# Turning the last batch's q and k by DMA in a fused attention and feed-forward kernel

## The chip, the core and the metric

The program runs on one core of one Trainium2 chip. Its time is device microseconds from start to end of one execution. The kernel before takes 698.06 us, the median of 3 runs (697.01 to 699.1). The profile below is of one further execution, which took 696.34 us in all; the span from its first to its last recorded instruction is 694.5 us, and the 1.84 us between the two lie around the span.

## What is computed

Four batches of 8 heads, 576 positions, head size 64. A position bias goes through a small two-layer network; then softmax attention; the result is reshaped to 2304 tokens of 512 numbers and goes through a feed-forward layer of 2048 with a leaky activation.

```python
def _attn_ref(q, k, v, w1, b1, w2):          # q, k, v: (4, 8, 576, 64)
    scores = 1 / np.sqrt(D) * np.matmul(q, k.transpose(0, 1, 3, 2))
    x = (np.log1p(np.abs(rel)) / psi_i)[..., None]      # (576, 576, 1)
    bias = np.maximum(x @ w1 + b1, 0.0) @ w2             # (576, 576, 8)
    scores = scores + bias.transpose(2, 0, 1)[None]
    attn = np.exp(scores - np.max(scores, axis=-1, keepdims=True))
    attn = attn / (np.sum(attn, axis=-1, keepdims=True) + 1e-09)
    return np.matmul(attn, v)

def _moe_ref(x, w_in, w_out, alpha):         # x: (2304, 512)
    h = x @ w_in                              # 512 -> 2048
    g = np.maximum(h, 0.0) + alpha * np.minimum(h, 0.0)
    return g @ w_out                          # 2048 -> 512
```

## The kernel before

**Precision.** A float32 number is kept as two float16 planes, a rounded high part and the rest, and a product of two such numbers is three float16 matmuls (high by high, high by low, low by high). Weights, feed-forward inputs and, for batches 1 to 3, also q, k, v and the attention weights are held in this form. Batch 0 is computed in float32.

**Stages.** `bias_tile` (L472) makes the bias of 16 positions at a time and stores it to the scratch tensor `scr` in HBM. `weights` (L658) loads and splits the feed-forward weights. `qk_turn` (L569) loads q and k of one batch and one half of its heads as rows (positions on the partitions) and turns them, so that the head dimension lies on the partitions. `v_rows` (L620) loads and splits v. `unit` (L779) is the attention of one pair of heads and 256 or 320 positions: scores (L612), add the bias and take the maximum (L823, DVE), exponential (L826, ACT), normalise into planes (L836 or L837, then L839), turn them by DMA (L842), multiply by v (L876) and write the result into a feed-forward input tile `x` (L902, L904). `chunk` (L912) takes 256 tokens through the feed-forward layer: first product into PSUM tile `H` (L954, 24 matmuls), activation (L961 on ACT, L962 on DVE), planes of it (L965, L966 or L967), second product into `O` (L973, 12 or 6 matmuls), scale and store (L935 to L943).

**q and k of batches 1 to 3, before.** `load_rows` (L523) issues five DMAs each for q and k into buffers of the class `five` (7 slots, 128 x 1280 float32). `qk_scales` (L548) finds the largest magnitude of each, by DVE (L554) or by ACT (L555, whose element-wise result is junk and is put into the buffer that the turned q and k will fill); TensorE turns the two maxima (L464) and spreads them over the partitions (L466); eight small DVE instructions (L559 to L566) make a power-of-two scale of them. Then, for each of q and k and each of two pairs of heads, TensorE turns five blocks of rows in float32 (L586, a group of five) into one PSUM tile, ACT writes the scaled high plane from PSUM (L592) and DVE the low plane (L593) into the buffer `qk` (3 slots). That is four groups for one half of the heads and eight for a batch.

**Order.** Nothing is scheduled when the program is built: `ISSUE` lists all steps of the program in one sequence, with the engine for those that have a choice (a suffix .1 or .2), `SLOT` gives each buffer its slot, and `IDLE` says before which steps how many matmuls with a zero operand (L1025, "fillers") are put into TensorE's queue. Each engine executes its part of the list strictly in order. All DMAs but one are issued from SP's queue, so a DMA that waits for its data holds up every DMA behind it. TensorE alternates between attention and the feed-forward layer from the second batch on; a feed-forward chunk can run when all attention units of its tokens are done.

Of the kernel before, what the change touches and what calls it, by code (L numbers as in the profile page):

```python
# [10 lines left out]
F16 = mybir.dt.float16  # L11
# [8 lines left out]
P = 128  # L20
# [122 lines left out]
"""  # L143
IDLE = """
7:9 108:4 115:1 73:4 35:11 444:2 59:1 168:1 94:1 101:4 657:6 45:1 66:4 229:2 122:1 934:1 650:4 622:2 636:1 129:3 608:1 671:3 150:4 643:1 136:3 692:1
699:5 678:1 287:2 685:2 495:5 713:2 720:6 543:3 537:6 557:3 329:1 568:2 774:2 802:4 426:1
"""

# [929 lines left out]
```

## Time and profile before

| | |
|---|---|
| median of 3 runs | 698.06 us (697.01 to 699.1) |
| the profiled execution | 696.34 us, span 694.5 us |
| TensorE (PE) busy | 665.5 us, 96% of the span |
| VectorE (DVE) busy | 496.4 us, 71% |
| ScalarE (ACT) busy | 399.1 us, 57% |
| GpSimd (POOL) busy | 180.7 us, 26% |
| DMA, share of 16 engines | 77.5% |
| granted TensorE clock | 0.999 |

A busy share is a mean over stages. In this program the stages differ: in the first 180 us bias, weights and batch 0 are made, until some 590 us attention and feed-forward work are mixed, and the rest is feed-forward alone. So the profile is read by stretch, and for each stretch by the chain of waits. Matmuls overlap in the pipeline, so the mean time of one matmul row is longer than what it adds to the path; the pieces of the chain of waits show the latter.

### The profile page before, as it was taken

How to read it: one execution, taken by the hardware profiler on the slowest of the kernel's cores; microseconds unless marked ns; L12 is line 12 of the kernel's file. 1: busy time of each engine (PE TensorE's matmuls, PEld its weight loads, DVE VectorE, ACT ScalarE, POOL GpSimd, SP SyncE). 2: the span in 40 equal slices, each digit the busy share in tenths (PEclk: the TensorE clock that was granted, in tenths of full speed). 3: DMA queues.
4: the chain of work that ended last, by engine and by line, in shares of the span. 5: the costliest groups of instructions: out<-in, count | busy, mean ns of one | idle time of the engine just before them, and what ended most of it. 6: DMA issues, size and time to landing. Idle time of an engine off the chain costs nothing.

```text
span 694.5 us, 15288 instructions
## 1 busy us (share of the span) xinstructions
PE 665.5 (96%) x5737; PEld 421.7 (61%) x5737; DVE 496.4 (71%) x1208; ACT 399.1 (57%) x820; POOL 180.7 (26%) x244
## 2 busy tenths in 40 slices
PE   7998898999999999999999999999999999999997
PEld 2544444556666657666665766666666667666664
DVE  4999999998788878897786787867686564132221
ACT  3579999896756766656646665454565333222311
POOL 1445245441233122111214211302121131111120
PEclk9999999999999999999999999999999999999999
DMA  8999998868589999999998999799997863100000
GB/s 198 267 291 321 302 323 282 283 178 200 119 209 182 200 192 233 186 221 221 197 236 200 209 199 191 158 212 184 175 218 167 172 134 61 33 31 1 31 1 32
DMA packets 234342, 125.89 MB, mean 181 GB/s; under 512 B 202636, under 2 KB 202652, under 8 KB 234268
## 3 DMA queue, kind: packets, MB, share of 16 engines
q1 hardware_dynamic: 234136, 124.91, 77.5%
q8 instruction: 45, 0.74, 0.4%
q14 instruction: 29, 0.24, 0.1%
q10 hardware_dynamic: 132, 0.00, 0.0%
HBM read 73.88 MB, written 15.61 MB: 129 GB/s over the span
## 4 chain that ended last, share of the span: by engine, by line
PE 72%; DVE 12%; DMA 6%; issue 4%; ACT 3%; POOL 2%; SPq 0%; ACTq 0%; DVEq 0%; POOLq 0%
PE H L954 25%; PE O L973 24%; PE S L612 7%; PE A L876 6%; DMA at<-a 2%; PE A L884 2%; PE S L586 2%; PE S L503 1%; DVE fg L823 1%; DVE five L682 1%; DVE wout L682 1%; DVE qk L593 1%; DVE at L482 1%; PE S L855 1%; DMA five<-in_k_dram 1%
## 5 line engine op out<-in xcount | busy, mean ns | idle before, releaser
L954 PE MATMUL H<-x,win 128*128 128x256 f16 x1728 | 200.7, 273 | 0.7 <-DVE mg L962 0.5
L973 PE MATMUL O<-wout,mg 128*128 128x512 f16 x864 | 197.7, 379 | 0.3 <-DVE mg L966 0.3
L954 PEld LDWEIGHTS <-win 128*128 128x128 f16 x1728 | 166.5, 98 | 33.9 <-issue 6.8
L962 DVE SCALAR_TENSOR_TENSOR mg<-H,sm,mg 128x256 f32<-128x256 f32 x144 | 66.8, 479 | 105.7 <-ACT mg L961 105.5
L961 ACT ACTIVATE mg<-H,sm 128x256 f32<-128x256 f32 x144 | 64.8, 470 | 134.1 <-PE H L954 115.2
L973 PEld LDWEIGHTS <-mg 128*128 128x128 f16 x864 | 82.6, 98 | 92.5 <-issue 3.8
L826 ACT ACTIVATE fg<-fg,st 128x576 f32<-128x576 f32 x144 | 110.6, 769 | 29.0 <-DVE st L823 23.8
L823 DVE CUSTOM_DVE_ANT_0 fg<-S,fg 128x576 f32<-128x576 f32 x127 | 93.6, 751 | 15.7 <-PE S L612 14.6
L967 POOL TENSOR_TENSOR mg<-mg 128x512 f16<-128x512 f32 x41 | 50.1, 1222 | 114.1 <-ACT mg L965 45.2
L839 DVE SCALAR_TENSOR_TENSOR a<-fg,st,a 128x576 f16<-128x576 f32 x71 | 59.5, 840 | 19.8 <-POOL a L836 9.9
L836 POOL TENSOR_SCALAR a<-fg,st 128x576 f16<-128x576 f32 x41 | 32.8, 802 | 136.5 <-DMA at<-a 77.1
L612 PE MATMUL S<-qk 64*128 64x288 f16 (+1 forms) x696 | 56.6, 285 | 2.2 <-DVE qk L593 2.2
L876 PE MATMUL A<-at,five 128*64 128x256 f16 (+3 forms) x720 | 51.5, 288 | 0.6 <-DMA at<-cst 0.6
L829 POOL TENSOR_SCALAR st<-st 128x2 f32<-128x2 f32 (+1 forms) x54 | 17.3, 320 | 123.1 <-ACT fg L826 118.9
L612 PEld LDWEIGHTS <-qk 64*128 64x128 f16 (+1 forms) x720 | 33.0, 96 | 23.1 <-issue 17.7
L876 PEld LDWEIGHTS <-five 128*64 128x64 f16 (+1 forms) x720 | 36.1, 109 | 15.0 <-issue 11.9
L485 ACT ACTIVATE at<-cst 128x528 f32<-128x528 f32 (+17 forms) x54 | 33.8, 659 | 10.2 <-PE S L503 7.4
L503 PE MATMUL S<-at,w2b 128*32 128x79 f32 (+37 forms) x462 | 32.9, 334 | 5.5 <-ACT at L485 1.9
L1025 PE MATMUL H<-sm 128*128 128x512 f16 x121 | 36.3, 412 | 0.9 <-DVE sm L413 0.9
L965 ACT ACTIVATE mg<-mg 128x512 f16<-128x512 f32 x40 | 24.9, 624 | 17.9 <-DVE mg L962 6.6
L839 DVE SCALAR_TENSOR_TENSOR cst<-fg,st,cst 128x576 f16<-128x576 f32 x37 | 32.0, 864 | 3.0 <-ACT cst L837 3.0
L488 POOL TENSOR_SCALAR at<-cst,npsi 128x416 f32<-128x416 f32 (+15 forms) x28 | 23.1, 827 | 41.6 <-PE S L503 24.0
(158 smaller groups left out, 902.3 us busy)
## 6 DMA issues: line engine op xcount, KB each, us to landing
fg<-scr SPq DMA_DIRECT2D x64, 576.0 KB, 4.6
scr<-fg SPq DMA_DIRECT2D x36, 295.5 KB, 4.9
x<-in_moe_w_in_dram SPq DMA_DIRECT2D x11, 512.0 KB, 5.6
x<-in_moe_w_out_dram SPq DMA_DIRECT2D x10, 512.0 KB, 5.7
fg<-scr SPq DMA_DIRECT2D x32, 144.0 KB, 4.1
out_dram<-mg SPq DMA_DIRECT2D x18, 256.0 KB, 2.7
five<-in_q_dram SPq DMA_DIRECT2D x32, 128.0 KB, 3.8
five<-in_k_dram SPq DMA_DIRECT2D x32, 128.0 KB, 3.3
```

What stands on the lines that cost most here:

```text
L503: nc.tensor.matmul(ps.t[32 * gl:32 * gl + 32, c:n], lhsT=w2b, rhs=x, start=True, stop=True)
L612: return [(lambda a, dst=dst, zq=zq, zk=zk, i=i: nc.tensor.matmul(dst(a), lhsT=tr16(qt)[at, 0, pr, zq, lo:lo + n], rhs=tr16(qt)[at, 1, pr, ...
L823: V(lambda x=x, sl=sl, st=st, ls=ls: nc.vector.tensor_tensor_reduce(out=in_halves(ls[x]()), in0=halves(sl[x].t), in1=in_halves(ls[x]()), s ...
L826: A(lambda x=x, st=st, ls=ls: nc.scalar.activation(ls[x](), ls[x](), AF.Exp, bias=st.t[:, x:x + 1], scale=-1.0, accum_out=st.t[:, 2 + x:3 ...
L839: V(lambda x=x, rec=rec, ls=ls, a16=a16: nc.vector.scalar_tensor_tensor(a16.t[:, 640:640 + S], ls[x](), rec(), a16.t[:, 0:S], op0=ALU.mult ...
L876: nc.tensor.matmul(ps.t[64 * hh:64 * hh + 64, 0:w], lhsT=v5[0:hi, zv, n, 2 * pr + hh, :], rhs=at16(at)[0:hi, 5 * za + n, 320 * hh:320 * hh ...
L954: nc.tensor.matmul(hb.t[:, f, :], lhsT=win[:, fp, zw, kb, P * f:P * f + P], rhs=x[:, zx, kb, :], start=(n == 0), stop=(n == 11))
L961: A(lambda f=f: nc.scalar.activation(gf(f), hb.t[:, f, :], AF.Copy, scale=cu[:, f:f + 1]), 470, ky, [hb, t_sig], [(g, f)])
L962: V(lambda f=f: nc.vector.scalar_tensor_tensor(gf(f), hb.t[:, f, :], cs[:, f:f + 1], gf(f), op0=ALU.mult, op1=ALU.max), 475, ky, [hb, t_si ...
L967: ("POOL", 1210, lambda: nc.gpsimd.tensor_tensor(gv(1), g.t, gv(0), op=ALU.subtract))], ky, [g, (gg, 0)], [(gg, 1)], tag="g1", cont=True)
L973: nc.tensor.matmul(ob.t[:, t, :], lhsT=gg.t[:, zg, f, P * t:P * t + P], rhs=wout[:, fp, zw, f, :], start=(first and f == 0 and (zg, zw) == ...
L1025: nc.tensor.matmul(idle, lhsT=zero.broadcast_to((P, P)), rhs=zero.broadcast_to((P, 512)), start=True, stop=True)
```

## The change

For batch 3 alone, `qk_turn` no longer uses TensorE to turn q and k. The new `qk_planes` takes two more buffers of the class `five`, one for q and one for k, and lets ACT (L577) write the high plane and DVE (L578) the low plane from the rows as they were loaded, one instruction each of 128 x 1280 for q and for k. Ten DMA transposes (L582), five each, then turn blocks of 128 (or, the last one, 64) rows of these planes, 512 columns wide, into the buffer `qk`. The junk of the maximum on ACT (L555) goes into the plane buffer. For the two halves of the heads this is 40 TensorE transposes, 8 ACT and 8 DVE instructions of 128 x 576 less, and 4 ACT and 4 DVE instructions of 128 x 1280 and 20 DMAs in SP's queue more. The scale, the three products and the layout of `qk` stay as they were.

`ISSUE`, `SLOT` and `IDLE` are all new: the whole sequence differs, not only the rows of batch 3. The lines after the insertion are numbered 21 higher (L612 is L633, L842 is L863, L954 is L975, L973 is L994).

```diff
-0 2 9 10 3 11 4 13 12 15 5 14 19 104 106 6 7 107.1 8 16 205 206 193 105.2 108 113 114.1 20 21 22 111.2 17 71.1 194 112 23 115 24 25 48 207 26 70.2 27
...
-7:9 108:4 115:1 73:4 35:11 444:2 59:1 168:1 94:1 101:4 657:6 45:1 66:4 229:2 122:1 934:1 650:4 622:2 636:1 129:3 608:1 671:3 150:4 643:1 136:3 692:1
...
+20:13 108:7 664:1 35:1 45:3 671:2 657:1 168:1 73:4 52:1 66:5 80:3 629:3 122:6 87:3 650:1 615:3 608:3 143:2 636:3 129:4 150:2 692:8 643:4 727:3 699:3
...
-    def qk_scales(st, tr, key):
+    def qk_scales(st, tr, key, planes=None):
...
-            junk = lambda tr=tr, j=j: tr.t[:, j].rearrange("p a n -> p (a n)").bitcast(F16)[:, 0:1280]
+            junk = (lambda j=j: planes[j].t.bitcast(F16)[:, 0:1280]) if planes else (lambda tr=tr, j=j: tr.t[:, j].rearrange("p a n -> p (a n)").bitcast(F16)[:, 0:1280])
...
+    def qk_planes(st, tr, key):
+
+        planes = [Buf(c_stage) for _ in range(2)]
+        sc2, tok = qk_scales(st, tr, key, planes)
+        for j in range(2):
+            p5 = lambda j=j: planes[j].t.bitcast(F16).rearrange("p (r c z n) -> p r c z n", r=5, c=2, z=2)
+            src = lambda j=j: st[j].t.rearrange("p (r c n) -> p r c n", r=5, c=2)
+            sv = sc2[:, j:j + 1]
+            A(lambda p5=p5, src=src, sv=sv: nc.scalar.activation(p5()[:, :, :, 0], src(), AF.Copy, scale=sv), 1350, key, [st[j], tok], [(planes[j], 0)])
+            V(lambda p5=p5, src=src, sv=sv: nc.vector.scalar_tensor_tensor(p5()[:, :, :, 1], src(), sv, p5()[:, :, :, 0], op0=ALU.mult, op1=ALU.subtract),
+              1550, key, [st[j], tok, (planes[j], 0)], [(planes[j], 1)])
+            for r in range(5):
+                lo = 64 if r == 4 else 0
+                TR(lambda e, j=j, r=r, lo=lo, p5=p5: e.dma_start_transpose(out=tr16(tr)[:, j].rearrange("p c z n -> p (c z) n")[:, :, P * r:P * r + P - lo],
+                                                                          in_=p5()[lo:P, r].rearrange("p c z n -> p (c z n)")),
+                   (P - lo) * 512 * 2, key, [planes[j]], [(tr, (j, r))])
+
...
+        if b in (3,):
+            qk_planes(st, tr, key)
+            qkt[b, hf] = tr
+            return
```

The order in which the built programs' instructions stand shows the change at three places. A number behind a name is the buffer (`five_74` and so on are slots of the class `five`, `at_84` and `at_85` the two buffers for turned attention weights, `a_87`, `a_88` and `cst` the three for the planes before they are turned, `qk_82` one of three for turned q and k).

TensorE, before: the last of the eight groups of batch 3 (k, second half of the heads), between a second and a first feed-forward product.

```order
L973 LDWEIGHTS mg
L973 MATMUL O_63<-wout,mg 128x512
L586 MATMUL S_65<-cst,five_74 128x128 x4
L586 MATMUL S_65<-cst,five_74 128x64
L954 LDWEIGHTS win
L954 MATMUL H_67<-x_93,win 128x256
```

TensorE, after: none of these groups is left for batch 3; what is left of its preparation on this engine are the turn of the two maxima (L464) and the spreading (L466), here L464 for the second half of the heads, between a second feed-forward product and scores of batch 2.

```order
L994 MATMUL O_63<-wout,mg 128x512
L464 MATMUL A_66<-cst,sm 2x128
L633 LDWEIGHTS qk_83
L633 MATMUL S_65<-qk_83 128x288
L633 LDWEIGHTS qk_83
L633 MATMUL S_64<-qk_83 128x288
```

What moved: 40 rows L586 are gone from TensorE's queue, and the first-half pair L464 and L466 stands three first products (L975), five second products of 12 (L994) and three sets of scores ahead of the second-half L464.

SP, before: what follows the last loads of k (batch 3, second half of the heads).

```order
L530 DMA five_77<-in_k_dram 64x4x64
L796 DMA fg<-scr_106 128x2x576
L842 DMA_TRANSPOSE at_84<-a_87 128x10x128
L796 DMA fg<-scr_106 128x2x576
L809 DMA fg<-scr_107 64x576 x2
L842 DMA_TRANSPOSE at_84<-a_88 128x10x128
L842 DMA_TRANSPOSE at_84<-cst 128x10x128
```

SP, after: most of the ten new transposes of the first half of the heads, among the last loads of k for the second half and the transposes and bias loads (L817) of batch 2's attention.

```order
L582 DMA_TRANSPOSE qk_82<-five_75 128x4x128
L530 DMA five_79<-in_k_dram 128x4x64
L582 DMA_TRANSPOSE qk_82<-five_76 128x4x128
L530 DMA five_79<-in_k_dram 128x4x64
L863 DMA_TRANSPOSE at_85<-cst 128x10x128
L582 DMA_TRANSPOSE qk_82<-five_76 128x4x64
L582 DMA_TRANSPOSE qk_82<-five_75 128x4x128 x2
L530 DMA five_79<-in_k_dram 64x4x64
L817 DMA fg<-scr_106 128x2x576
L582 DMA_TRANSPOSE qk_82<-five_76 128x4x128
L582 DMA_TRANSPOSE qk_82<-five_75 128x4x64
```

What moved: three more of the ten follow at once, the second of them the last that reads `five_75`; the ten for the second half of the heads stand further down, singly or in pairs among 24 transposes of attention weights. The last loads of batch 3's k, which stood earlier, ahead of attention transposes of batch 2 (the piece above), now stand among the new transposes.

ACT, before: the last maximum on ACT (batch 3, second half), whose junk goes into `qk_82`.

```order
L826 ACTIVATE fg,st_98<-fg,st_98 128x576 x2
L837 ACTIVATE cst<-fg,st_95 128x576
L965 ACTIVATE mg<-mg 128x512
L961 ACTIVATE mg<-H_67,sm 128x256 x2
L837 ACTIVATE a_87<-fg,st_102 128x576
L555 ACTIVATE qk_82,sm<-five_77 128x1280
```

ACT, after: the maximum of q, second half, whose junk goes into `five_75`, the buffer that the first half's transposes of k read.

```order
L858 ACTIVATE a_88<-fg,st_104 128x576
L982 ACTIVATE mg<-H_67,sm 128x256
L555 ACTIVATE five_75,sm<-five_77 128x1280
L982 ACTIVATE mg<-H_67,sm 128x256
L923 ACTIVATE x_91<-A_66 128x128
```

What moved: L555 waits in ACT's queue until the five transposes out of `five_75` are done, with the second half of a feed-forward activation (L982) behind it.

## Rows read from the trace of the kernel before

**Rows 1.** Busy time by stretch; us, then busy (x instructions), clock, DMA share, GB/s.

```profile
core 0: us, PE busy (x) PEld busy (x) DVE busy (x) ACT busy (x) POOL busy (x), PEclk, DMA share, GB/s
0.00:180.00 180.00, 159.90 (x1558) 88.61 (x1560) 160.29 (x397) 143.13 (x260) 66.02 (x92) 1.00 0.87 260
240.00:320.00 80.00, 76.22 (x642) 50.58 (x641) 66.02 (x163) 52.87 (x110) 17.59 (x24) 1.00 1.05 205
320.00:592.00 272.00, 271.86 (x2360) 179.19 (x2359) 193.43 (x461) 141.05 (x320) 62.46 (x86) 1.00 0.89 183
```

**Rows 2.** Chain that ended last, 325 to 440 us: start, us, what.

```profile
by line: PE H L954 35.2%; PE O L973 32.2%; PE S L612 14.6%; PE A L876 12.4%; PE S L586 5.0%; PE A L466 0.5%; PE A L464 0.2%
...
333.35 1.43 PE S L586 x10
...
342.18 2.73 PE H L954 x24
344.90 0.84 PE S L612 x12
...
385.94 2.28 PE A L876 x30
...
390.94 2.59 PE O L973 x12
393.53 0.64 PE S L586 x5
...
432.31 0.79 PE S L586 x5
```

**Rows 3.** TensorE's waits, 190 to 345 us: us in total, times, longest.

```profile
PE S L612 <- DVE qk L593: 2.2, 3, 1.2
PE A L876 <- DMA at<-cst: 0.6, 1, 0.6
```

**Rows 4.** One line's instructions: ns least/median/most, first and last start; transposes, bias loads.

```profile
L842 SPq DMA_TRANSPOSE at<-a x81: 1205/1419/3203, 201.4 to 591.6; - x81
...
DMA to landing us min/median/max: 2.9/3.7/6.4
...
L796 SPq DMA_DIRECT2D fg<-scr x64: 359/530/1718, 59.2 to 550.7; - x64
```

**Rows 5.** The copies into planes of v, and the maximum on ACT.

```profile
L641 ACT ACTIVATE five<-five,sm x6: 1348/1352/1362, 67.2 to 412.0; 128x1280 f16<-128x1280 f32 x6
L642 DVE SCALAR_TENSOR_TENSOR five<-five,sm,five x6: 1529/1542/1624, 83.4 to 470.5; 128x1280 f16<-128x1280 f32 x6
...
L555 ACT ACTIVATE qk<-five x7: 1254/1271/1273, 167.5 to 373.7; 128x1280 f16<-128x1280 f32 x7
```

**Rows 6.** First and last of the eight small DVE instructions of one scale.

```profile
330.25 0.15 DVE L559 TENSOR_SCALAR sm<-A 128x2 f32<-128x2 f32 x1
...
332.71 0.15 DVE L566 TENSOR_SCALAR sm<-sm 128x1 f32<-128x1 f32 x1
```

**Rows 7.** DMA queue, 400 to 480 us, then 60 to 100 us: packets, MB, share.

```profile
q1 hardware_dynamic: 34190, 14.67, 88.2%
...
fg<-scr SPq DMA_DIRECT2D x9, 576.0 KB, 4.3
fg<-scr SPq DMA_DIRECT2D x6, 144.0 KB, 3.1
out_dram<-mg SPq DMA_DIRECT2D x3, 256.0 KB, 3.7
at<-a SPq DMA_TRANSPOSE x18, 3.7
at<-cst SPq DMA_TRANSPOSE x8, 3.5
...
q1 hardware_dynamic: 5354, 12.13, 90.6%
```

More of the change, by code (lines that the diff above doesn't have):

```diff
@@ L34 @@
 ISSUE = """
[91 rows of a table removed]
[91 rows of a table added]
 """
 SLOT = """
[15 rows of a table removed]
[15 rows of a table added]
 """
 IDLE = """
-7:9 108:4 115:1 73:4 35:11 444:2 59:1 168:1 94:1 101:4 657:6 45:1 66:4 229:2 122:1 934:1 650:4 622:2 636:1 129:3 608:1 671:3 150:4 643:1 136:3 692:1
-699:5 678:1 287:2 685:2 495:5 713:2 720:6 543:3 537:6 557:3 329:1 568:2 774:2 802:4 426:1
+20:13 108:7 664:1 35:1 45:3 671:2 657:1 168:1 73:4 52:1 66:5 80:3 629:3 122:6 87:3 650:1 615:3 608:3 143:2 636:3 129:4 150:2 692:8 643:4 727:3 699:3
+678:1 489:2 685:1 495:3 512:4 720:1 706:5 557:1 534:1 329:2 565:2 745:1 582:4 788:3 767:1
 """
@@ L552, in qk_scales @@
         for j in range(2):
-            junk = lambda tr=tr, j=j: tr.t[:, j].rearrange("p a n -> p (a n)").bitcast(F16)[:, 0:1280]
+            junk = (lambda j=j: planes[j].t.bitcast(F16)[:, 0:1280]) if planes else (lambda tr=tr, j=j: tr.t[:, j].rearrange("p a n -> p (a n)").bitcast(F16)[:, 0:1280])
             pl.op([("DVE", 1500, lambda j=j: nc.vector.tensor_reduce(mx[:, j:j + 1], st[j].t, AX.X, ALU.max, apply_absolute_value=True)),
                    ("ACT", 1450, lambda j=j, junk=junk: nc.scalar.activation(junk(), st[j].t, AF.Abs, accum_out=mx[:, j:j + 1]))],
-                  key, [st[j]], [(tok, j), (tr, j)], tag="mq")
+                  key, [st[j]], [(tok, j), planes[j] if planes else (tr, j)], tag="mq")
         ps = allmax(mx, 2, key, tok)
```

211 rows, old and new, of tables (ISSUE, SLOT) are left out of this document.

## The prediction

> **What bounds the kernel now.** First the busy times by stretch, because a share over the whole span mixes stages [rows 1]. From 320 to 592 us TensorE is busy 271.86 of 272 us, and the stretch ends only when TensorE has got through its queue. From 240 to 320 us it misses 3.78 us, and there the share of the DMA engines stands at 1.05. In the first 180 us it misses 20.1 us; VectorE is as busy there as TensorE (160.29 against 159.90), and neither bounds alone. The granted clock is 1.00 in all of these. Then the chain that ended last, for 325 to 440 us, where batch 3 is prepared [rows 2]: the reader is to see that every piece is TensorE's, with no DMA and no other engine between. So in this stretch an instruction taken off TensorE's queue is worth its piece of the chain, as long as nothing comes late for it. Third, TensorE's waits from 190 to 345 us [rows 3]: scores wait 2.2 us for the low planes of turned q and k, and the product with v 0.6 us for turned weights. Last come durations of single lines and the transfers of two stretches [rows 4 to 7].
>
> **What is removed from TensorE.** The turns (L586) of batch 3 are eight groups of five, and all of them stand in this chain: two pieces of two groups (the one of 1.43 us is shown), and four single groups of 0.64 to 0.79 [rows 2]. Together they are 5.0% of the 115 us from 325 to 440, 5.7 us. They are next to nothing but other TensorE work, so the whole of it goes: **-5.7**. At 0.79 for each of the eight it would be 6.3, at 0.64 5.1; these are the bounds. The turn and the spreading of the two maxima (L464, L466) stay.
>
> **What is removed from and added to ACT and DVE.** Eight copies of 128 x 576 on each go, and four of 128 x 1280 on each come. The new ones have the form of v's copies, 1.35 us on ACT and 1.54 on DVE [rows 5], so 5.4 and 6.2 us in all. From 320 to 592 us ACT is busy 141 and DVE 193 of 272 us [rows 1]. The difference in load is below what this slack holds, even if the removed ones had cost nothing: 0. Cover: TensorE's 272 us of work; where one of them is waited for, its length is in the next step.
>
> **The new wait for the junk of a maximum.** The maximum of q, second half, on ACT (L555) now writes into the plane buffer `five_75`, which it may do only when five transposes have read it. TensorE's turn of the maxima (L464, second half) needs that maximum, and behind it stand all scores. So I add up the path from TensorE's spreading for the first half (L466) to this second L464. The eight small DVE instructions took 2.6 us from first to last [rows 6]. Then come two copies on ACT, 2 x 1.35, and the last one on DVE, 1.54 [rows 5]: 6.8 us so far. Then SP: in its queue nine transposes and four other DMAs stand from the first transpose of the burst to the last out of `five_75`. An issue took 1.42 us in the middle case for a transpose and 0.53 for a bias load, and a transpose landed 3.7 us after its issue [rows 4]: 9 x 1.42 + 4 x 0.53 + 3.7 = 18.6. Last, L555 itself, 1.27 [rows 5]. Sum 26.7 us.
>
> Against that, TensorE has to do between the two steps three first products at 2.73, five second ones at 2.59 and three sets of scores at 0.84 [rows 2], 23.7 us, with some 0.4 for two small steps of v's maximum: 24.1. So it waits **+2.6**. Bounds: with issues of 1.205 and 0.359 and a landing of 2.9 [rows 4] SP's part is 15.2 and the wait 0; with one issue of 3.2 and the longest landing of 6.4 it is 7.1. The middle rows are taken, since thirteen issues in a row average out. Behind L555 in ACT's queue stands the second half of a feed-forward activation (L982), for which the next second product waits; that one stands behind L464 anyway. If the first half's scale is made late, the cover is the same, since both ends move with it. The 26.7 us assume that the burst finds SP free.
>
> **Twenty transposes more for SP.** From the first to the last of them SP issues 45 transposes and 22 other DMAs, 45 x 1.42 + 22 x 0.53 = 76 us [rows 4]. TensorE's work over the same piece of its queue is, by the pieces of the chain, some 87 us, so SP is 87% issuing; I count issue alone as load, and a DMA that waits for its data adds to it. All turned weights of the last units go through that queue.
>
> **And for the DMA engines.** From 60 to 100 us there are plain transfers only: 12.13 MB at a share of 90.6%, which is 0.335 MB per us. From 400 to 480 us 14.67 MB took 88.2% of 80 us, 70.6 us; the plain ones in it (9 x 0.590 + 6 x 0.147 + 3 x 0.262 MB = 7.0 MB) would be 20.9 us of that, and the other 7.7 MB, 26 transposes, 49.7 us [rows 7]. That is 1.9 us each or 6.5 us per MB. The new ones move 16 x 131 KB and 4 x 66 KB, 2.36 MB: 15 us in 87. The share of this stretch thereby goes from 0.9 to some 1.07, what 240 to 320 us had, where TensorE missed 3.78 of 80 us [rows 1]. So late transposes should cost between the 0.6 us that TensorE waited for one [rows 3] and 3.8; I take **+1.2**, nearer to the lower end, because the last-batch stretch has more feed-forward work between attention units.
>
> The Trainium skill has two rules here. "Advanced Engine Details and Errata", section "X-Bar Transpose (TRN2)", says that transposes by DMA are as fast as regular ones on this chip. By it the new ones would take 2.36 MB / 0.335 = 7 us, the share would stay below 1 and the term be 0.6, the sum 0.6 us lower. The rows speak against it: transposes there took some twice the time per byte.
>
> **What the order moves.** In the table before, batch 3's rows were loaded, and its maxima made, inside the stretch 190 to 345 us; now the last loads stand among the first new transposes and the turns by TensorE are gone from there. This relieves the stretch in which TensorE waited 2.2 us for low planes and 0.6 for a transpose [rows 3]. I take half, **-1.4**, with 0 and the 3.78 us missed from 240 to 320 [rows 1] as bounds. One zero matmul (L1025) more, 121 to 122, is under 0.5 us and put at 0. The first 180 us hold no part of batch 3 and are only listed anew, with some relu tiles moved from DVE and POOL to ACT: 0, and 3 us to either side, a sixth of the 20.1 us missed there.
>
> **Sum.** -5.7 + 2.6 + 1.2 - 1.4 = -3.3. The profiled execution took 696.34 us, which is 1.72 below the median shown, 698.06, and 1.84 above its span of 694.5. So the span would be 691.2, the execution 693.0, and the median **694.8**. A measurement of this kernel can tell some 0.3%, 2.1 us, from no change; the sum is beyond that, barely.
>
> **Rival 1: the full saving.** The burst finds a faster queue (the lower bound, wait 0), no transpose comes late, the stretch before is relieved: -5.7 - 1.4 = -7.1, or -5.7 with a less relieved stretch; 691 to 692.4. For it: TensorE had 0.14 us idle in 272 [rows 1], though 26 transposes ran in 80 us of it. Against it: the burst's sum has no slack, and five transposes out of one buffer must end.
>
> **Rival 2: the waits eat it.** The burst is at its upper bound (7.1) with the other terms as above: -5.7 + 7.1 + 1.2 - 1.4 = +1.2, 699.3; or the wait is 4 to 5 and the stretch is not relieved: 698. For it: the issue of a transpose was up to 3.2 us long, and SP waits in order. Against it: that needs most of the thirteen issues, or the landing, to be slow.
>
> **Rival 3: the DMA path becomes the bound, slower.** Place: the units of batches 2 and 3 in the piece with the new transposes. Six products with v stand there, and each needs turned weights that wait in SP's queue behind up to three new transposes. Three times 1.42 of issue is 4.3 us; with a slack of some 2 us each product would be 2 us late: 6 x 2 = 12, less the saving of 5.7 and 1.4, and with no burst wait: +5, 703. It decides from where SP's issuing and its waits together pass TensorE's 87 us, which is 11 us above the 76. For it: the share 1.07. Against it: 240 to 320 us had the same share, and one wait for a transpose in TensorE's queue, of 0.6 us [rows 3].
>
> The Trainium skill speaks for this rival: "VectorE: DVE Perf Modes", section "The three transpose paths", gives 390 ns for a 128 x 128 block of 16 bits on TensorE and 1309 ns by DMA, and its rules prefer TensorE where PSUM can take the result. An estimate by that page: 16 x 4 + 4 x 4 = 80 blocks at 1309 ns are 105 us in a stretch of 87. The trace disagrees as to the price: a transpose of some ten blocks landed 3.7 us after its issue [rows 4].
>
> **Rival 4: the new order costs elsewhere.** The first 180 us come out at the 3 us bound or a bit more and the last batch saves nothing: some 702. No row speaks for it but the 20.1 us of idle that depend on order.
>
> That the change does nothing, because the turns are hidden anyway, is excluded by the chain: they are on it.
>
> **How the numbers follow.** Forecast (693 to 696) 0.37; rival 1 (690 to 692.9) 0.23; rival 2 (696 to 700.1) 0.23; rival 3 (701 to 705) 0.12; rival 4 0.05. The range from 689.5 to 701 leaves out rival 3's and 4's greater part and a saving in the first 180 us of more than a us. Faster by over 0.3% is below 696.0: forecast and rival 1, 0.60; within 0.3%, 696.0 to 700.2: 0.23; slower: 0.17.
>
> **What would show it.** In the profile of the changed kernel the chain of waits has no turn of q and k of batch 3, and TensorE's busy time is near 660 us: that is the first term. A wait of TensorE's L464 for the ACT maximum of the second half, and of that for transposes, once, of 0 to 7 us, somewhat after 400 us, is the second. The third is in waits of the product with v for turned weights in the last batch, each under 1 us; several of 2 us or more would be rival 3. The fourth is an idle time from 240 to 320 us below 3.78. The forecast is wrong if the first 180 us miss more than 23 or less than 17 us, or if TensorE waits in a place that none of these names.

## The result

The changed kernel takes 706.75 us, the median of 4 runs (704.85 to 708.6), against 697.53 (696.71 to 699.1) for the kernel before: 1.0129 times as long, 95% interval 1.0096 to 1.0162. That is slower by 9 us, where 694.8 was forecast and 701 was the end of the range. The profiled execution took 708.6 us, its span 706.8 (before: 694.5).

Busy times of the changed kernel by stretch, in the columns of [rows 1]; the last two rows are pieces of the third:

```profile
0.00:180.00 180.00, 157.53 (x1519) 84.98 (x1520) 156.59 (x391) 148.85 (x270) 60.76 (x88) 0.99 0.87 255
240.00:320.00 80.00, 78.11 (x662) 51.22 (x661) 62.15 (x162) 45.85 (x97) 21.48 (x25) 1.00 1.02 208
320.00:592.00 272.00, 261.93 (x2265) 172.17 (x2264) 190.29 (x451) 144.91 (x320) 65.59 (x84) 0.98 0.94 187
425.00:441.00 16.00, 11.57 (x67) 6.23 (x66) 7.55 (x20) 4.57 (x11) 3.89 (x5) 0.68 0.96 194
490.00:546.00 56.00, 50.83 (x474) 34.05 (x473) 37.49 (x87) 25.63 (x59) 16.85 (x19) 1.00 1.05 213
```

TensorE misses 10.1 us from 320 to 592, where it missed 0.14. It misses 1.9 instead of 3.8 from 240 to 320, and 22.5 instead of 20.1 in the first 180 us. Its busy time is 666.5 us, 1 us more than before, though 40 turns are gone: from 430 to 440 us it worked at half clock (below), and in the first 180 us the mean clock was 0.99. Its longest waits from 420 to 550 us (us in total, times, longest):

```profile
PE A L464 <- ACT five L555: 4.2, 1, 4.2
PE A L897 <- DVE x L925: 1.8, 1, 1.8
PE S L633 <- DVE st L844: 1.7, 2, 1.5
```

The first is the wait that the prediction worked out, 4.2 us where it had 2.6. SP's queue around it (start, us; several of a kind in one row):

```profile
418.22 3.97 SPq L582 DMA_TRANSPOSE qk<-five  x3
422.23 0.65 SPq L530 DMA_DIRECT2D five<-in_k_dram  x1
422.97 0.55 SPq L817 DMA_DIRECT2D fg<-scr  x1
423.57 6.46 SPq L582 DMA_TRANSPOSE qk<-five  x5
430.14 1.33 SPq L863 DMA_TRANSPOSE at<-cst  x1
431.52 1.56 SPq L863 DMA_TRANSPOSE at<-a  x1
```

TensorE in the same piece (idle time before a row in brackets, with what ended it):

```profile
424.69 2.75 PE L994 MATMUL O<-wout,mg 128*128 128x512 f16 x12
431.63 0.37 PE L464 MATMUL A<-cst,sm 128*2 128x128 f32 x1 [4.18 <-ACT five L555]
431.93 1.62 PE L633 MATMUL S<-qk 64*128 64x288 f16 x12
...
434.31 3.55 PE L897 MATMUL A<-at,five 128*64 128x256 f16 x30 [0.25 <-DVE sm L559]
437.79 3.80 PE L994 MATMUL O<-wout,mg 128*128 128x512 f16 x12
441.52 1.95 PE L897 MATMUL A<-at,five 128*64 128x256 f16 x30
443.40 0.91 PE L633 MATMUL S<-qk 64*128 64x288 f16 x12
```

After the wait the same work takes longer: the scores 1.62 us against 0.91, the product with v 3.55 against 1.95, the second product 3.80 against 2.75, 3.4 us in these three. The granted clock, the third number from the end of each row:

```profile
424.00:428.00 4.00, 3.45 (x20) 1.70 (x18) 1.88 (x2) 0.47 (x1) 0.57 (x1) 1.00 1.03 232
428.00:430.00 2.00, 0.00 (x0) 0.00 (x0) 0.00 (x0) 0.00 (x0) 0.00 (x0) 0.92 0.37 74
430.00:440.00 10.00, 8.12 (x51) 4.93 (x52) 4.67 (x16) 3.79 (x9) 3.04 (x4) 0.50 1.00 212
440.00:444.00 4.00, 4.00 (x48) 2.49 (x48) 2.21 (x8) 0.89 (x4) 0.85 (x2) 1.00 1.32 209
```

The clock went to the lower of its two levels (1.2 GHz) while TensorE stood idle, and came back at 440 us.

### The profile page after: what moved, and what is told of

Read it like the earlier page. It is cut to its first block, busy times and chain, and to the rows that moved or that the text cites. A ratio compares the mean times of both kernels' runs of the same rounds, so it can differ in the third digit from the quotient of the medians.

```text
span 706.8 us, 15203 instructions
## 1 busy us (share of the span) xinstructions
PE 666.5 (94%) x5698; PEld 420.3 (59%) x5698; DVE 496.3 (70%) x1214; ACT 406.1 (57%) x827; POOL 171.4 (24%) x227
## 4 chain that ended last, share of the span: by engine, by line
PE 60%; DVE 12%; DMA 12%; ACT 5%; SPq 5%; issue 4%; POOL 1%; ACTq 0%; POOLq 0%; DVEq 0%
PE O L994 22%; PE H L975 22%; PE A L897 6%; PE S L633 5%; DMA at<-a 4%; DVE fg L844 3%; SPq L530 3%; DMA scr<-fg 2%; ACT fg L847 2%; DMA fg<-scr 1%; DMA at<-cst 1%; PE S L607 1%; SPq L582 1%; DVE five L703 1%; DVE win L703 1%
## 5 line engine op out<-in xcount | busy, mean ns | idle before, releaser
L975 PE MATMUL H<-x,win 128*128 128x256 f16 x1728 | 200.6, 273 | 1.8 <-DVE mg L983 1.0
L994 PE MATMUL O<-wout,mg 128*128 128x512 f16 x864 | 198.9, 381 | 0.8 <-DVE st L844 0.4
L975 PEld LDWEIGHTS <-win 128*128 128x128 f16 x1728 | 167.0, 98 | 35.4 <-issue 7.9
L982 ACT ACTIVATE mg<-H,sm 128x256 f32<-128x256 f32 x144 | 63.5, 470 | 137.4 <-PE H L975 119.4
L994 PEld LDWEIGHTS <-mg 128*128 128x128 f16 x864 | 82.9, 98 | 94.0 <-issue 6.3
L844 DVE CUSTOM_DVE_ANT_0 fg<-S,fg 128x576 f32<-128x576 f32 x119 | 88.1, 750 | 19.2 <-PE S L633 17.2
L988 POOL TENSOR_TENSOR mg<-mg 128x512 f16<-128x512 f32 x39 | 48.1, 1238 | 141.5 <-DVE mg L986 63.6
L860 DVE SCALAR_TENSOR_TENSOR a<-fg,st,a 128x576 f16<-128x576 f32 x70 | 57.7, 827 | 25.2 <-POOL a L857 13.4
L857 POOL TENSOR_SCALAR a<-fg,st 128x576 f16<-128x576 f32 x40 | 34.3, 858 | 108.2 <-DMA at<-a 53.3
L897 PE MATMUL A<-at,five 128*64 128x256 f16 (+3 forms) x720 | 53.2, 294 | 4.1 <-DVE x L925 3.8
L633 PE MATMUL S<-qk 64*128 64x288 f16 (+1 forms) x648 | 55.1, 288 | 1.7 <-DVE st L844 1.7
L850 POOL TENSOR_SCALAR st<-st 128x2 f32<-128x2 f32 (+1 forms) x51 | 18.0, 353 | 145.3 <-ACT fg L847 135.7
L897 PEld LDWEIGHTS <-five 128*64 128x64 f16 (+1 forms) x720 | 37.9, 111 | 18.5 <-issue 15.4
L633 PEld LDWEIGHTS <-qk 64*128 64x128 f16 (+1 forms) x720 | 32.3, 97 | 22.7 <-issue 17.3
L485 ACT ACTIVATE at<-cst 128x448 f32<-128x448 f32 (+17 forms) x58 | 35.7, 651 | 9.6 <-PE S L503 5.7
L503 PE MATMUL S<-at,w2b 128*32 128x79 f32 (+40 forms) x420 | 32.7, 342 | 4.5 <-ACT at L485 2.3
L858 ACT ACTIVATE a<-fg,st 128x576 f16<-128x576 f32 x30 | 23.1, 771 | 18.7 <-DMA at<-a 15.3
L923 ACT ACTIVATE x<-A 128x192 f16<-128x192 f32 (+3 forms) x48 | 12.9, 285 | 32.2 <-PE A L897 31.9
```

The source lines that it names most:

```text
L485: nc.scalar.activation(hb.t[:, 0:wd], R[:, 0:wd], AF.Relu, bias=PSI[:, g:g + 1], scale=1.0)
L633: return [(lambda a, dst=dst, zq=zq, zk=zk, i=i: nc.tensor.matmul(dst(a), lhsT=tr16(qt)[at, 0, pr, zq, lo:lo + n], rhs=tr16(qt)[at, 1, pr, ...
L844: V(lambda x=x, sl=sl, st=st, ls=ls: nc.vector.tensor_tensor_reduce(out=in_halves(ls[x]()), in0=halves(sl[x].t), in1=in_halves(ls[x]()), s ...
L860: V(lambda x=x, rec=rec, ls=ls, a16=a16: nc.vector.scalar_tensor_tensor(a16.t[:, 640:640 + S], ls[x](), rec(), a16.t[:, 0:S], op0=ALU.mult ...
L897: nc.tensor.matmul(ps.t[64 * hh:64 * hh + 64, 0:w], lhsT=v5[0:hi, zv, n, 2 * pr + hh, :], rhs=at16(at)[0:hi, 5 * za + n, 320 * hh:320 * hh ...
L975: nc.tensor.matmul(hb.t[:, f, :], lhsT=win[:, fp, zw, kb, P * f:P * f + P], rhs=x[:, zx, kb, :], start=(n == 0), stop=(n == 11))
```

## The experiments

All ratios are to the kernel before on the same chip.

**1. Fillers in the wait.**

```diff
+    idle_a = cA.tiles[0]
...
+            for _ in range(18 if o.seq == 1818 else 0):
+                nc.tensor.matmul(idle_a, lhsT=zero.broadcast_to((P, P)), rhs=zero.broadcast_to((P, 512)), start=True, stop=True)
```

> The changed kernel with 18 matmuls with a zero operand (128 x 512, like the fillers, but into the PSUM tile A) ahead of TensorE's turn of the maxima for batch 3, second half. In the profile of the changed kernel TensorE waits 4.2 us there for the maximum on ACT, and then the granted clock stands at 0.50 for some 10 us, in which scores, a product with v and a second product take 3.9 us longer than elsewhere. Theory (the idle engine is what lowers the clock): the fillers take some 0.23 us each, lie within the wait and cost nothing, the clock stays at 1.00, and the time falls from 706.75 by 3.9 us to 703, some 1.008 times the kernel before. Rival (the clock falls there for another reason, or zero operands don't hold it): the clock still falls, and the time stays at 706 to 708, 1.013.

Measured: 703.66 us, 1.0113 (1.0091 to 1.0136). The clock stayed at 1.00 to 438 us. But TensorE then waited 2.1 us for the next product with v, and behind that wait worked at half clock for some 3 us. The theory holds for the clock at that place; the time can't be told from 1.0129, so what the fillers are worth is not shown.

**2. and 3. The wait itself taken away,** by the maximum on DVE (`1816.1` becomes `1816` in `ISSUE`) or by the order of the ten transposes (their steps alone, the steps between them left out):

```diff
-1801 1792 1796 1802 1799 1793 1803 1795 1800 1794
+1801 1802 1799 1803 1800 1792 1796 1793 1795 1794
```

> The changed kernel with one instruction on another engine: the maximum of q, batch 3, second half, is made by DVE (L554) instead of ACT (L555), so no junk is written into the buffer that the first half's transposes read. Theory (that write is what TensorE waited for): the wait of 4.2 us and the 3.9 us of half clock behind it are gone, for 1.5 us more on DVE, which has slack there; 706.75 - 8.1 = 698.7, within 0.3% of the kernel before, and the granted clock is 1.00 from 425 to 441 us. Rival (the burst of transposes in SP's queue is what holds up the stretch, whatever waits for it first): the wait moves on to scores or to the product with v, and the time stays above 704.

> The changed kernel with the ten transposes of the first half in another order at the same ten places of SP's queue: first the five that read the buffer into which the junk of the next maximum goes, then the other five. Theory (the length of the burst up to the last of these five is the wait): five transposes at some 1.3 us leave that path, 6.5 us against a wait of 4.2, so the wait and the half clock are gone: 706.75 - 8.1 = 698.7, as with the maximum on DVE. Rival (the landing of transposes under a DMA share near 1 decides, not their place): a wait of 2 us or more stays, and with it the half clock; 703 or more.

Measured: 1.0168 (1.0145 to 1.0192) and 1.0145 (1.0123 to 1.0166): no gain. The wait at L464 is gone in both, and another begins some 6 us later. TensorE with the maximum on DVE:

```profile
425.96 0.27 PE L464 MATMUL A<-cst,sm 128*2 128x128 f32 x1
...
429.50 2.76 PE L994 MATMUL O<-wout,mg 128*128 128x512 f16 x12
440.33 3.54 PE L897 MATMUL A<-at,five 128*64 128x256 f16 x30 [8.06 <-DVE x L925]
443.81 1.60 PE L633 MATMUL S<-qk 64*128 64x288 f16 x12
```

Pieces of the chain of waits of that run that lead to it:

```profile
429.62 2.16 SPq L863
...
431.82 3.57 DMA at<-a
...
435.57 0.03 POOL a L857
...
436.40 0.83 POOL st L850
...
439.09 0.26 DVE x L925
...
440.33 3.54 PE A L897 x27
```

A transpose of attention weights that stood behind the ten is issued late, at 431.8 us; its landing, 3.57 us, is no longer than the 3.7 of [rows 4]. POOL (L857) waits for it, since it may only then write into that plane buffer again; POOL's next instruction (L850) and with it DVE come late, and DVE empties the one PSUM tile A (L925) late. Without the twenty (run 4) the same transpose was issued at 422.6 us and POOL wrote at 426.4 instead of 435.6. In the changed kernel the wait at L464 had stood in front of this one. Both theories of these two runs fell; the rival of the first was right.

**4. Leaving the transposes out,** all (shown) or one half (`hf == 0 or`, `hf == 1 or`):

```diff
-                TR(lambda e, j=j, r=r, lo=lo, p5=p5: e.dma_start_transpose(
+                TR(lambda e, j=j, r=r, lo=lo, p5=p5: True or e.dma_start_transpose(
```

> The changed kernel without the twenty new transposes (the planes are made as before, turned q and k of batch 3 are never written, the scores read what the buffers hold). The last runs showed that the wait at TensorE's L464 only stood in front of another: with it gone, the next product with v but one stood idle for 8 us, since the transposes of its attention weights are behind the ten new ones in SP's queue. Theory (SP's queue with the twenty transposes is the whole loss after 400 us: 4.2 us of wait, 3.9 of half clock and 5.2 idle from 490 to 546): TensorE has no wait over 0.6 us from 400 to 600, and the time is 13 us under that of the changed kernel (1.0129 times the kernel before), so some 0.994 to 0.995 times the kernel before. Rival (the new order of the rest is as much to blame): 1.003 or more.

> The changed kernel without the ten transposes of the first half of the heads alone (turned q and k of that half are never written). Theory: the burst is gone, so neither L464 nor the product with v behind it waits: 4.2 and 3.9 us less, and the 5.2 us idle from 490 to 546 us stay: 1.0129 - 0.0116, some 1.001. Rival (the DMA engines are simply full from 400 to 546 us): TensorE still waits for a product with v near 430 us, 1.006 or more.

> The changed kernel without the ten transposes of the second half of the heads alone. Theory: the wait at L464 and the half clock stay (8.1 us), and of the 5.2 us idle from 490 to 546 us most goes, as the transposes of attention weights there no longer stand behind new ones: 1.0129 - 0.007, some 1.006. Rival (those waits come from the order of the units or from a few long landings, not from these ten): 1.011 or more.

Measured: 0.9958 (0.9928 to 0.9989) without the twenty, 1.0022 (1.0004 to 1.0041) without the first ten, 1.0052 (1.003 to 1.0074) without the second, all three times as the theory had them, within the intervals. In detail it was less exact: without the first ten TensorE misses 2.7 us from 490 to 546, not 5.2. So the twenty cost 1.0129 - 0.9958, 12 us; alone, the second ten cost 4.5 us and the first 6.6. Without the twenty, TensorE from 320 to 592 us, as above:

```profile
320.00:592.00 272.00, 271.28 (x2356) 178.16 (x2354) 196.09 (x466) 149.39 (x329) 66.64 (x85) 1.00 0.90 184
```

What the second ten do shows in the chain of waits from 490 to 546 us. In the kernel before and without the twenty it is made of TensorE's pieces alone; in the changed kernel transposes of attention weights lead, with POOL, ACT and DVE between them (shares of these 56 us; the view breaks the line off):

```profile
by line: DMA at<-a 33.7%; issue 10.4%; DMA at<-cst 9.1%; PE A L897 7.4%; PE H L975 4.9%; PE S L633 4.1%; ACT fg L847 4.1%; POOL a L857 4.0%; DVE fg L844 3.7%; DVE a L860 3.0%; DVE five L663 2.6%; ACT five L662 2.4%; POOL cst L857 2.0%; SPq 
```

**5. The gain alone:** the kernel before without batch 3's turns.

```diff
-                    for r in range(5):
+                    for r in range(0 if b == 3 else 5):
```

> The kernel before without the 40 turns (L586) of batch 3's q and k on TensorE (ACT and DVE still copy what the PSUM tiles hold). It measures the gain alone, with nothing in its place. Theory (the first term of the sum): TensorE's queue bounds that stretch, so 5.7 us go, 0.992 times the kernel before. Rival (something else is late by about as much as TensorE was busy): 0.997 or more.

Measured: 1.0012 (0.9988 to 1.0036). The theory fell: 5.7 us of TensorE's work gone, and at most 0.8 us of time. The same stretch:

```profile
320.00:592.00 272.00, 266.47 (x2320) 175.57 (x2318) 195.92 (x465) 141.18 (x322) 61.66 (x87) 1.00 0.90 183
```

TensorE misses 5.5 us of 272 instead of 0.14. Its waits from 320 to 490 us:

```profile
PE S L612 <- DVE qk L593: 1.3, 3, 0.5
PE H L954 <- DVE mg L962: 1.3, 2, 1.1
PE S L612 <- DVE st L823: 1.2, 1, 1.2
PE O L973 <- ACT mg L935: 0.8, 1, 0.8
PE O L973 <- POOL mg L967: 0.6, 1, 0.6
```

Five kinds of waits for DVE, ACT and POOL, none over 1.2 us: in this order the other engines were only just ahead of TensorE, and what it was spared it waited. The first kind, 1.3 of the 5.2 us, is for copies of turned q and k, which this run still makes and the change does without.

**6. Issues or bytes.** Twenty small transposes, the four of q in one, and the four of q and of k in one:

```diff
-    in_=p5()[lo:P, r].rearrange("p c z n -> p (c z n)")),
+    in_=p5()[lo:lo + 32, r].rearrange("p c z n -> p (c z n)")),
...
+    (lambda e, j=j, p4=p4: e.dma_start_transpose(out=flat16(tr, j)[:, 0:2048].rearrange("p (q n) -> p q n", n=P), in_=p4()[:, 0:2048])) if r == 0 else
...
```

The first pair of lines belongs to the small ones, the last line to the eight; the rest of these edits, above all the scores' reading of the other layout, is left out here.

> The changed kernel with each of the twenty new transposes cut to 32 rows (128 or 64 before), so that most of turned q and k of batch 3 is not written: as many issues in SP's queue at the same places, but 0.65 MB instead of 2.36. The runs without transposes put the price of the twenty at 1.0129 - 0.9958, 12 us. Theory A (issue time in SP's one queue is the price, some 1.3 us an issue whatever its size): 1.009 or more, and TensorE still waits near 430 us. Theory B (the time that the DMA engines take for the bytes is the price): 3/4 of it goes, 1.000 or less.

> The changed kernel with the four full transposes of q of each half of the heads made in one of 128 x 2048 (turned q then lies in another order, and the scores of batch 3 read it so): 14 issues instead of 20, the same bytes. Theory A (the issues are the price): three issues leave the burst, 4 us, and three the second half, so a third of the 12 us goes: some 1.007. Theory B (the bytes are the price): 1.012 or more, as the larger one lands later.

> The changed kernel with eight transposes in place of twenty: the four full blocks of q, and of k, of each half of the heads in one of 128 x 2048, and the last 64 rows in one of 64 x 512. Turned q and k of batch 3 lie in blocks of 128 positions, and TensorE makes the scores of batch 3 in pieces of 512 and 64 columns instead of twice 288. The run with 14 issues went from 1.0129 to 1.006, with the same bytes. Theory A (SP's issues are the price): 0.6 us each over twenty, so twelve less give 7 us: 1.003 or less, and the wait near 430 us with its half clock is gone. Theory B (large transposes land late enough to take the place of many): no better than the run with 14, 1.006 or more.

Measured: 1.011 (1.0086 to 1.0135) with 0.65 of 2.36 MB; with all bytes 1.006 (1.0042 to 1.0078) in 14 issues and 1.0005 (0.9984 to 1.0026) in eight. Theory A was right each time: the price goes with the number of transposes. SP's issue times (least/median/most, ns) and the landing, of the changed kernel:

```profile
L582 SPq DMA_TRANSPOSE qk<-five x20: 1188/1266/2090, 411.9 to 505.7; - x20
...
DMA to landing us min/median/max: 2.4/2.6/5.4
```

With 32 rows each:

```profile
L582 SPq DMA_TRANSPOSE qk<-five x20: 1162/1237/1981, 410.4 to 501.6; - x20
```

With eight, the four large ones, and from a second answer the four small ones:

```profile
L583 SPq DMA_TRANSPOSE qk<-five x4: 1857/2500/3657, 412.5 to 469.6; - x4
...
DMA to landing us min/median/max: 4.4/4.4/5.8
...
L584 SPq DMA_TRANSPOSE qk<-five x4: 1189/1250/1365, 418.3 to 479.0; - x4
```

At the medians, twenty are 25 us of SP's time and eight 15. Ten us less for SP made the kernel 8.6 us shorter (1.0129 - 1.0005). TensorE's scores in pieces of 512 and 64 take 0.84 us a set in this run's chain of waits, as before [rows 2], so the other pieces are no gain of their own. A fixed time of every transpose on the DMA engines, whatever its bytes, would also go with the number. Against it stands that the landings hardly moved: from 410 to 550 us attention's transposes out of `a` and `cst` took 4.2 and 4.0 us to land in the changed kernel, 4.0 and 3.7 without the twenty.

**7. The ten spread out.** With the maximum on DVE, two transposes at a time between those of attention weights, k's first; the two maxima no longer claim the plane buffers for their junk (steps in their order, others left out):

```diff
-1801 1812 1792 1813 1642 1796 1802 1799 1814 1793 1803 1795 1800 1794 1631 1645 1628
+1801 1812 1802 1813 1642 1799 1803 1814 1631 1800 1792 1645 1793 1796 1628 1795 1794
```

> The changed kernel with the maximum of q, second half, on DVE (so that nothing waits for a junk write), and the first half's ten transposes no longer in a row: two at a time between the four transposes of attention weights that stood behind them. Theory (place in the one queue decides: what stood behind ten now stands behind two, four, six and eight): TensorE's wait of 8 us near 430 us, seen with the maximum on DVE, falls below 3 and with it the half clock goes, 1.004 to 1.007. Rival (the three buffers for planes of attention weights go round through this queue, so each added transpose costs its issue wherever it stands): 1.011 or more.

Measured: 1.0153 (1.0136 to 1.017). The rival was right as to the time. Its reason, that the attention weights' planes with their three buffers go round through this queue, shows in the chain of waits of this run (lines are 3 higher here, the new transposes are L585):

```profile
426.47 1.56 SPq L585
...
428.08 1.26 SPq L585
...
429.39 3.67 DMA at<-a
...
433.25 0.76 POOL a L860
...
435.01 5.83 DMA at<-a
```

Two new transposes stand ahead of one of attention weights; POOL writes the next planes when it has landed, and TensorE's next product with v waits 5.0 us for the transpose of these. That one also landed late, 5.83 us after its issue. That every issue costs the same wherever it stands is not shown.

**8. Eight, with the maximum on DVE.**

> The kernel with eight transposes and, as in an earlier run, the maximum of q, second half, on DVE instead of ACT, so that no junk is written over the planes. If the junk write still makes TensorE wait with only four issues in the burst: 1 to 3 us less than with eight alone. If the transposes of attention weights come late there anyway: the same, within 0.3%.

Measured: 0.9991 (0.9972 to 1.001), the same as with eight alone within the intervals. With a short burst the junk write has no part that can be measured. Neither of the two beats the kernel before by what can be told.

**9. The first 180 us.** The order of before for the first steps, and the changed one behind it, with 1010 steps, with 620, and with 620 on the kernel with eight issues.

> The changed kernel with its list's first 1010 steps in the order of the kernel before (with that list's fillers and, for the buffers of these steps, its slots); after them the changed list goes on with what is left. That is some 180 us: bias, weights and batch 0. Theory (the new order of the first 180 us costs some 4 us: TensorE misses 22.5 us there against 20.1, and works at half clock from 10 to 13 us): the first 180 us are those of before, and the time falls by 4 us to 702.7, 1.007 times the kernel before, with the wait and the half clock after 425 us left as they are. Rival (what is lost there is not on the path, since the units that follow wait for something else): 706 to 708.

> The changed kernel with the first 620 steps in the order of the kernel before (some 110 us; at this place the two lists have done the same but for 7 steps, so the seam that cost the run with 1010 steps its waits at 195 us is smaller). Theory (some of the 2.4 us by which TensorE missed more of the first 180 us come from the new order there): 1 to 2 us less, 1.010 to 1.012. Rival (the first 110 us are alike): 1.013, or more if the seam costs.

> The kernel with eight transposes and the first 620 steps in the order of the kernel before. The same head on the changed kernel gave 1.0123 against 1.0129. If the first 110 us are as long in both orders: the same as with eight alone, within 0.3%; if the new order loses there: 1 to 2 us less.

Measured: 1.0311 (1.0289 to 1.0334), 1.0123 (1.0108 to 1.0138) and 1.0022 (1.0004 to 1.0041). The first is inconclusive: at its seam TensorE waited 3.8 us for a maximum at 201 us and worked at half clock behind it, which neither order has. The other two show no gain from the old order of the first 110 us; the intervals overlap. What the new order loses between 110 and 180 us no run tells apart; the traces say something of it (next section).

## Why the prediction was wrong

The forecast was 3.3 us less than before, the result 9 us more: the sum was 12 us off. The twenty transposes cost 12 us, where the second and third terms together had 3.8 for them; that is 8 us of the error. Without the twenty the run is 2.9 us below the kernel before, where the first and fourth terms together had 7.1; that is the other 4.2.

**The gain of 5.7 us** was sized by TensorE's pieces of the chain, and these were right: they are what left its queue. "The whole of it goes" does not follow from them. A chain that shows one engine only says that nobody was late in that run, not by how much: run 5 puts this term at 0 in the old order (0.8 us at most). In the new order, without the transposes, TensorE does stay busy after 320 us without the turns (271.28 of 272), yet that run is 2.9 us below the kernel before (0.9958), not 7.1. The traces place the rest in **the first 180 us, put at 0**. TensorE's work behind 180 us, in the kernel before and without the twenty:

```profile
180.00:694.50 514.50, 505.64 (x4183) 333.12 (x4179) 336.10 (x812) 255.96 (x560) 114.65 (x152) 1.00 0.75 154
180.00:693.40 513.40, 504.43 (x4181) 332.53 (x4179) 338.35 (x824) 257.05 (x558) 110.60 (x139) 1.00 0.75 156
```

Less the 5.7 us of turns, the first would be 499.9; the second is 4.5 us more. So by 180 us the new order had got less done, and the changed kernel had done no more (x1519 in both). An estimate from these rows is a loss of 3 to 4.5 us; the lower end, because these two executions differ by 1.1 us only and the medians by 2.9. It is one execution each, with a clock of 1.00 and 0.97 in the first 180 us, and no run changes that stretch alone: this part is not shown by an experiment.

**ACT and DVE** were sized rightly: the new copies took 1.35 and 1.55 us.

**The wait for the junk write** was found at its place, with its cover (24.1 us) right and its path 28.3 us (from 403.3 to 431.6) where 26.7 was worked out: 4.2 us for 2.6, inside the bounds. Two things were left out. The half clock behind it added 3.4 us. And the term was no price of its own: with that wait taken away, the next product with v waited 8 us (runs 2 and 3), for the same burst.

**Late transposes, +1.2,** is the term that failed most. It was priced by the share of the DMA engines, between two waits of the kernel before; SP's load, 87% by issue alone, was worked out beside it and given no price. The terms for the burst and for lateness together were 3.8; the twenty cost 12. From 412 to 506 us the share was 0.95, not 1.07; with eight transposes it was 1.03, and they cost nothing that can be told. The price is not the bytes (with little over a quarter of them: 1.011) nor, in the middle case, a late landing (run 6), though single landings of 5 to 6.5 us stand in the chains. It is the round of three plane buffers through one queue in order: issues ahead of an attention transpose delay the buffer, then POOL or ACT, then DVE, which also empties TensorE's PSUM tile (the chains of runs 2 and 7). For the burst this is shown; for the second ten it is read from the chain in run 4. More than a third of it is in no burst: the second ten, one or two at a time, cost 4.5 us.

**The order, -1.4,** was about half that: from 180 to 320 us TensorE misses 3.1 us for 3.8. The reading behind it was wrong for the second half of batch 3: its maximum on ACT was made at 373.7 us [rows 5], behind the stretch that was to be relieved. In the first 180 us TensorE misses 2.4 us more, inside the limit that the prediction set (22.5, not over 23); but a miss does not tell what is left to do.

**The rivals.** Rival 3, given 0.12, comes nearest, at the place named: products with v that are held up by new transposes in SP's queue. Its path is only half of it: in the changed kernel they wait not for turned weights but for the PSUM tile, which DVE empties late. Its 12 us equal the price of the twenty, but by luck: it had six products 2 us late each, no wait at L464 and no half clock. Its 703 was too low because it took off the whole 7.1. The row that was held against it, one wait of 0.6 us in [rows 3], was read from a queue without the added issues and had nothing to say of them. The rule of the Trainium skill that spoke for it ("VectorE: DVE Perf Modes", section "Rules for kernel authors": TensorE where PSUM can take the result) was right here in its direction for twenty transposes; with eight, no difference from the kernel before can be told (1.0005). Its price by blocks was not right: eight with the same blocks cost 8.6 us less than twenty.

## What to carry to other kernels

Before a piece of the bounding engine's work is counted as gain, take it out and run: only then does it show by how much the other engines are ahead. In an in-order DMA queue count issues, and follow the buffers that go round through it; make transposes as large as the operands allow before moving them from TensorE. When the order of a whole program changes, compare what is left to do at a seam, not only the idle time before it. Price a wait of the matrix engine with what it does to its clock.

## What the runs showed of the hardware

A transpose's issue hardly depends on its rows: 1.24 us with 32 rows and 1.27 with 128 or 64 at 512 columns. One of four times the columns took 2.5 us, twice as long, and landed in 4.4 us instead of 2.6.

TensorE's granted clock fell to half while it stood idle from 427.4 to 431.6 us in the changed kernel, and stayed there for 8 us of work behind the wait. Behind a wait of 1.8 us before 505.5 us in the same run it was still 1.00; behind one of 2.1 us in run 1 it fell.
